# Attention and SoLU feed-forward in one kernel: the order of the PV matmuls, and mask matmuls over the whole array

## The chip, the cores and the metric

The kernel runs on one core of a Trainium2 chip. The metric is the device time of one execution in microseconds. Three executions took 211.36, 210.92 and 211.4 us; their median is 211.36. A core has the engines TensorE (PE, matmul), VectorE (DVE), ScalarE (ACT), GpSimd (POOL) and SyncE (SP, which here issues DMA transfers).

## What is computed

The reference has two parts. The first is attention with a block mask, for 4 batches, 8 heads, 768 tokens and a head size of 64:

```
scores = q @ k.T / sqrt(64)
mask: blocks of 32 tokens; a pair of blocks is kept if the blocks are at most one apart,
      if either is the first or the last block, or if the key block is among
      the three sampled blocks of the query block
attn = softmax(where(mask, scores, -1e9)); x = attn @ v
```

The second part takes the heads of a token side by side (512 numbers) and computes

```
h = x @ w_in                      # 512 -> 1024
solu = h * softmax(h)
out = layernorm(solu) * g @ w_out # 1024 -> 512
```

## The kernel before, in words

**Attention.** The 768 tokens of a head are six chunks of 128. Heads are worked in pairs. q and k are cast to bf16 and transposed, so that kT and qT hold the 64 head dimensions on partitions 0 to 63. On partitions 64 to 87 lie 24 more rows, one for each block: in kT a one-hot of the key's block, in qT the mask row of the query's block (0, or -30000 for a block that is left out). So a score matmul over 88 rows adds the mask by itself. These rows come from two small tiles that are made once at the start: `selq`, which says to which block each of the 768 tokens belongs, and `maskq`, the 24 x 24 mask of blocks. Two matmuls of line 353 spread the mask over tokens for the first head pair (24 columns of weights, 256 and 512 columns of data), and six of line 371 do it for all other tiles (128 columns of weights, 24 columns of data each). Both contract over the 24 blocks alone. The zeros and ones behind these tiles are written by memsets of VectorE at line 311.

A unit of attention (`attend`) is one batch, one head pair and one query tile of 256 queries. It has three steps. In each, four score matmuls (line 504, 256 columns each) fill an `sbank` of PSUM with the scores of four key chunks, and one instruction of ScalarE (line 515) takes the exponential of all 1024 columns into an `ex` tile [128 keys, 4 chunks, 256 queries]. Then three PV steps multiply by V. Step n has eight matmuls (line 525): for each of its four chunks m, and for each half a of the 256 queries, the weights are the 128 x 128 piece of `ex`, the moving data are the V tile of the chunk (64 values and a one for the sum, 65 columns), and the result is added to one of four places of 65 columns in an `mbank` of PSUM, one for each half and head. The V tiles of a batch lie end to end in `va` [128, 8 heads, 6 chunks, 65] in bf16, 130 bytes each. The chunk number runs over both heads of the pair: 4n + m from 0 to 11 is head (4n + m) // 6, chunk (4n + m) % 6. There are 48 units, so 576 score matmuls, 144 exponentials and 1152 PV matmuls. VectorE then divides by the sum (lines 536 and 539) into x.

**Feed-forward.** `feed` takes x of 256 tokens, transposes it (by DMA, or at line 555 on PE), computes h with matmuls of 512 columns (line 580), exponential (589), product and statistics on the other engines, transposes again, and multiplies by w_out with matmuls of 512 columns (line 636). VectorE or ScalarE scales the result (647, 650) and SP stores it.

**The order.** Nothing runs in the order of the loops. `op` records each piece of work with its engine, a guess of its cost, its dependencies and a due time. `Plan.run` then simulates the five engines with these guesses, and among the pieces that are ready on an engine takes the one that is due first; the pieces are emitted in the order of the simulated starts. A PV step enters as one piece of 8 x 0.0293 us, whatever its inner order. Memsets enter at 0.1 us each. Before the first matmul of line 580, idle time of PE in the simulation is filled with filler matmuls (line 703), at 0.9 of the idle time.

**Slots.** Scores rotate over two or three sbanks, PV and all other small results over two mbanks, `ex` over nine tiles.

Of the kernel before, what the change touches and what calls it, by code (L numbers as in the profile page):

```python
# [8 lines left out]
BF16 = mybir.dt.bfloat16  # L9
I32 = mybir.dt.int32  # L10
AX = mybir.AxisListType
ALU = mybir.AluOpType
ACT = mybir.ActivationFunctionType
# [9 lines left out]
def act_us(n, sbuf=False):  # L23
    return (n + 60 + (52 if sbuf else 0)) / 1200
# [31 lines left out]
class Plan:  # L56
# [14 lines left out]
    def op(self, eng, us, emit, deps=(), due=0.0, take=None, last_of=(), load=None, after=()):  # L71
        o = Op(eng, us, emit, deps, due, take, last_of, load, after)
        for d in {id(d): d for d in o.deps + o.after}.values():
            d.next.append(o)
            o.open += 1
        for a, name in o.last_of:
            a.held[name][0] += 1
        self.ops.append(o)
        return o
# [75 lines left out]
def kernel(  # L155
# [11 lines left out]
    nc = tc.nc  # L167

    B, H, S, D = q.shape
    BLK = 32  # L170
    NB = S // BLK
    NR = sampled_blocks.shape[1]
    P = 128
    NCH = S // P
# [10 lines left out]
    DM = D + NB  # L185

    const = ctx.enter_context(tc.tile_pool(name="const", bufs=1))
    psum = ctx.enter_context(tc.tile_pool(name="psum", bufs=1, space=PSUM))

    SPARE = 0.9  # L190
    NST, NKB, NEX, NX, NE, NSO, NSOT, NXT, NOT = 4, 3, 9, 6, 2, 3, 3, 2, 3

    def bufs(name, shape, dt, n):
# [3 lines left out]
    kT = bufs("kT", [P, NPR, 2, S], BF16, 2)  # L197
    qT = bufs("qT", [P, NPR, 2, S], BF16, 2)
    va = bufs("va", [P, H, NCH, D + 1], BF16, 2)
# [5 lines left out]
    exb = bufs("ex", [P, 4, TW], BF16, NEX)  # L205
# [37 lines left out]
    op = plan.op  # L243
# [3 lines left out]
    def bank(o, dt=FP32):  # L247
        t = mbank[o.slot]
        return t if dt == FP32 else t.bitcast(dt)
# [7 lines left out]
    def xbar_us(tiles):  # L257
# [6 lines left out]
        out=samp_i.rearrange("a b c -> a (b c)"),  # L264
        in_=bass.AP(tensor=_t32, offset=0, ap=[[2 * NR, NB], [1, 2 * NR]])), due=-100, load=0.01)
# [3 lines left out]
        out=g8, in_=moe_g_ln.rearrange("(c p) -> c p", p=P)), due=-99.5, load=0.01)  # L269
# [30 lines left out]


    oneh = const.tile([P, NCH, NB], BF16, name="oneh")
    selq = const.tile([NB, NCH, P], BF16, name="selq")
    static = const.tile([NB, NB], FP32, name="static")
    kbi = const.tile([NB, NB], I32, name="kbi")
    anyeq = const.tile([NB, NB], FP32, name="anyeq")
    maskq = const.tile([NB, NB], BF16, name="maskq")
    flat = lambda t: t.rearrange("p a b -> p (a b)")

    def fill(t, val, due):  # L310
        return op("DVE", 0.1, lambda o: nc.vector.memset(t, val), due=due)  # L311

    m1, oh1 = fill(onesf, 1.0, -2200), fill(oneh, 1.0, -2199)
    mid, stz, last = fill(ident, 0.0, -2198), fill(static, 0.0, -2197), fill(anyeq, 0.0, -2196)

    def sel(t, us, fill, base, cm, pat, deps, cmp=ALU.is_ge):
# [7 lines left out]
            due=-2194)  # L324

    stat = io
    for args in ((-NEG, 1, -1, [[1, NB]]), (-NEG, 1, 1, [[-1, NB]]), (0.0, -1, 1, [[0, NB]]),
                 (0.0, NB - 2, -1, [[0, NB]])):
        stat = sel(static, 0.12, *args, [stat, stz])
    for c in (0, NB - 1):  # L330
        stat = op("POOL", 0.08, lambda o, c=c: nc.gpsimd.memset(static[:, c : c + 1], 0.0), [stat], due=-2194)
    idf = op("DVE", 0.1, lambda o: nc.vector.tensor_copy(out=identf, in_=ident[0:KF, 0:KF]), [mids, stage[("k", 0, 1)]], due=15)
    for r in range(NR):
        last = op("DVE", 0.24, lambda o, r=r: nc.vector.scalar_tensor_tensor(
            out=anyeq, in0=kbi, scalar=samp_i[:, r, 0:1], in1=anyeq, op0=ALU.is_equal, op1=ALU.max),
            [last, io, samp_dma], due=-2089)
    mq = op("DVE", 0.24, lambda o: nc.vector.scalar_tensor_tensor(
        out=maskq, in0=anyeq, scalar=1.0, in1=static, op0=ALU.subtract, op1=ALU.mult), [last, stat], due=-2088)

    def selq_tr(o):  # L340
        for c in range(NCH):
# [1 line left out]
                             start=(c == 0), stop=(c == NCH - 1))  # L343

    sqt = op("PE", NCH * 0.056, selq_tr, [ohs, mids], due=-2190, take="m")
    sqs = op("ACT", 0.75, lambda o: nc.scalar.copy(out=flat(selq), in_=bank(sqt, BF16)[0:NB, 0:S]), [sqt],
             due=-2189, last_of=[sqt])


    krow = [op("DVE", 0.36, lambda o, hh=hh: nc.vector.tensor_copy(out=kT[0][D:DM, 0, hh, :], in_=flat(selq)), [sqs],  # L350
               due=(-2087.5, -2079.8)[hh]) for hh in range(2)]
    mps = lambda o: bank(o)[0:NB]
    mmq = [op("PE", (hi - lo) * 0.00043, lambda o, lo=lo, hi=hi: nc.tensor.matmul(  # L353
# [22 lines left out]
    for i in (1, 2, 0):  # L376
        filled["k"].append(op("ACT", 0.38, lambda o, i=i: nc.scalar.copy(
            out=kb[i][:, :, :, D:DM],
            in_=oneh.rearrange("p (o c) b -> p o c b", o=1).broadcast_to([P, 2, NCH, NB])), [ohs], due=-2075))
        filled["q"].append(op("DVE", 0.4, lambda o, i=i: nc.vector.tensor_copy(  # L380
            out=qb[i][:, :, :, D:DM],
            in_=bank(mmm)[:, 0 : NCH * NB].rearrange("p (o c b) -> p o c b", o=1, c=NCH)
            .broadcast_to([P, 2, NCH, NB])), [mmm], due=-2076, last_of=[mmm]))
    vones = [op("POOL", 0.3, lambda o, i=i: nc.gpsimd.memset(va[i][:, :, :, D : D + 1], 1.0), [stat],
                due=-1900 if i == 0 else 0) for i in range(2)]
# [3 lines left out]
        out=w_in_sb[:, c : c + 2], in_=moe_w_in.rearrange("(c p) f -> p c f", p=P)[:, c : c + 2]),  # L389
        [stage[("k", 0, 3)]], due=-2000 + c, load=3.2) for c in (0, 2)]  # L390
    w_out_load = []
    for i in range(3):
        w_out_load.append(op("SP", 0.5, lambda o, i=i: nc.sync.dma_start(
            out=hold[i], in_=moe_w_out.rearrange("(c p) d -> p c d", p=P)[:, 3 * i : min(3 * i + 3, KF)]),
            due=-43.4 + 0.1 * i, load=2.3, deps=w_in_load[:1], after=[stage[("v", 0, 3)]] + w_out_load[-1:]))
# [7 lines left out]
        out=w_out_sb[:, c, :], in0=w_out_f[c], scalar1=g_sb[:, c : c + 1], scalar2=None,  # L403
        op0=ALU.mult), [w_out_load[c // 3], gc], due=26) for c in range(KF)]
# [89 lines left out]
    def attend(b, t, pr, A):  # L494
        i = b % 2
        got, vc, later = ready[(b, pr)]
        need = [got[hh] + later.get((hh, min(t, 1)), []) for hh in range(2)]
        exs = []
        for n in range(3):
            def score(o, n=n):  # L500
                s = sbank[o.slot]
                for m in range(4):
                    hh, jc = divmod(4 * n + m, NCH)
                    nc.tensor.matmul(s[:, m, :], kT[i][0:DM, pr, hh, jc * P : (jc + 1) * P],  # L504
                                     qT[i][0:DM, pr, hh, t * TW : (t + 1) * TW],
                                     start=(m % 2 == 0), stop=(m % 2 == 1))

            so = op("PE", 4 * 0.1087, score, need[0] + (need[1] if n else []), due=A + 0.9 * n,
                    take="s")
            last_use.setdefault((b, pr), []).append(so)  # L510
            if n == 0 and 1 <= b < B - 1:

                l = NPR * t + pr
                plan.follow(stage[("kqv"[l % 3], b + 1, l // 3)], so)
            exs.append(op("ACT", act_us(1024), lambda o, so=so: nc.scalar.activation(  # L515
                out=exb[o.slot], in_=sbank[so.slot], func=ACT.Exp, scale=scale), [so], due=A + 0.9 * n,
                take="ex", last_of=[so]))
        pv0 = None
        for n in range(3):
            def pv(o, n=n, pv0=pv0):  # L520
                acc = bank(pv0 or o)[:, 0 : 4 * (D + 1)].rearrange("p (a h d) -> p a h d", a=2, h=2)
                for m in range(4):
                    hh, jc = divmod(4 * n + m, NCH)
                    for qt in range(2):
                        nc.tensor.matmul(acc[:, qt, hh, :],  # L525
                                         exb[exs[n].slot][:, m, qt * P : (qt + 1) * P],
                                         va[i][:, 2 * pr + hh, jc, :], start=(n + m + qt == 0),
                                         stop=(n == 2 and m == 3 and qt == 1), skip_group_check=True)

            pvo = op("PE", 8 * 0.0293, pv, exs + [vc], due=A + 2.2 + 0.9 * n, take=None if n else "m",  # L530
                     last_of=[exs[n]], after=[pv_last] if n else [])
            pv0 = pv0 or pvo
            pv_last = pvo
        last_use.setdefault(("pv", b, pr), []).append(pvo)
        acc = lambda: bank(pv0)[:, 0 : 4 * (D + 1)].rearrange("p (a h d) -> p a h d", a=2, h=2)
        rc = op("DVE", 0.18, lambda o: nc.vector.reciprocal(out=rb[o.slot], in_=acc()[:, :, :, D : D + 1]),  # L536
                [pvo], due=A, take="r")
        fresh = (b, t) not in x_of
        nrm = op("DVE", 0.41, lambda o: nc.vector.tensor_tensor(  # L539
            out=xb[x_of[(b, t)].slot][:, :, 2 * pr * D : (2 * pr + 2) * D].rearrange(  # L540
                "p a (h d) -> p a h d", h=2),
            in0=acc()[:, :, :, 0:D], in1=rb[rc.slot].broadcast_to([P, 2, 2, D]), op=ALU.mult),
            [rc] + ([] if fresh else [x_of[(b, t)]]), due=A,
            take="x" if fresh else None, last_of=[pv0, rc])
        if fresh:
            x_of[(b, t)] = nrm
        x_done.setdefault((b, t), []).append(nrm)
# [125 lines left out]
    for b in range(B):  # L673
        for pr in range(NPR if b == 1 else 0):

            for nm, t in (("k", kT), ("q", qT)):
                mask_rows[(nm, pr)] = op("DVE", 0.75, lambda o, t=t, pr=pr: nc.vector.tensor_copy(
                    out=t[1][D:DM, pr], in_=t[0][D:DM, 0]),
                    (krow if nm == "k" else list(qrow.values())) + w_in_load[:1] + (wo if pr > 1 else []),
                    due=Q[NPR + pr] - 5)  # L680
# [18 lines left out]
    with tc.manual_schedule():  # L699
        for o in order:  # L700
            if o.eng == "PE" and o.start <= begin:
                for _ in range(max(0, int((o.start - idle) * SPARE / (0.107 if o.start < COLD else 0.0535)))):
                    nc.tensor.matmul(flat(sbank[2])[:, 0:P], onesf, onesf, start=True, stop=True)  # L703
# [32 lines left out]
```

The softmax here doesn't subtract the row's maximum and nothing guards it: scores larger than these inputs give would overflow.

## Time and profile before

| what | value |
|---|---|
| median of three runs | 211.36 us |
| the profiled execution, its own time | 211.36 us |
| its span, first to last instruction | 209.6 us |
| PE busy, share of the span | 204.5 us, 98% |
| ACT busy | 174.1 us, 83% |
| DVE busy | 152.7 us, 73% |
| DMA queue of the loads and stores (q1), share of 16 engines' span | 77.8% |
| L525, PV matmuls | 1152, mean 194 ns each by the profile's modelled ends |
| L504, score matmuls | 576, mean 278 ns each |
| L371 and L353, mask matmuls | 6 and 2, mean 180 and 507 ns each |

How to read it. PE is the matmul part of TensorE, PEld its weight loads, which overlap the matmuls. The ends of matmuls are modelled and run past the start of the next one; what counts on PE is the distance from one start to the next. "L525" is line 525 of the kernel; a group is all instructions of a line with one operation. The chain of work that ended last starts from the last instruction and goes back, at each step, to what released it or to the instruction before it on its engine; its shares say on which engine the end of the kernel hangs. In the chain and in the timeline, "x24" says that 24 instructions of a group follow each other.

### The profile page before, as it was taken

How to read it: one execution, taken by the hardware profiler on the slowest of the kernel's cores; microseconds unless marked ns; L12 is line 12 of the kernel's file. 1: busy time of each engine (PE TensorE's matmuls, PEld its weight loads, DVE VectorE, ACT ScalarE, POOL GpSimd, SP SyncE). 2: the span in 40 equal slices, each digit the busy share in tenths (PEclk: the TensorE clock that was granted, in tenths of full speed). 3: DMA queues.
4: the chain of work that ended last, by engine and by line, in shares of the span. 5: the costliest groups of instructions: out<-in, count | busy, mean ns of one | idle time of the engine just before them, and what ended most of it. 6: DMA issues, size and time to landing. Idle time of an engine off the chain costs nothing.

```text
span 209.6 us, 5885 instructions
## 1 busy us (share of the span) xinstructions
PE 204.5 (98%) x2332; PEld 146.7 (70%) x2332; DVE 152.7 (73%) x361; ACT 174.1 (83%) x215; POOL 63.4 (30%) x131
## 2 busy tenths in 40 slices
PE   7999999999999999999999999999999999999993
PEld 6589998878667678677677767776676756454442
DVE  4767689887977978756866883858896659788720
ACT  6558999999999999988999999998998937456532
POOL 5143033305453162045331116052401111323220
PEclk9999999999999999999999999999999999999998
DMA  5999988269999799298999679799721874658562
GB/s 171 338 383 354 262 301 153 79 149 229 326 230 194 225 288 176 51 267 209 221 228 260 145 225 211 147 306 260 171 84 49 137 191 51 153 124 177 153 202 100
DMA packets 71375, 41.80 MB, mean 199 GB/s; under 512 B 54316, under 2 KB 66868, under 8 KB 71348
## 3 DMA queue, kind: packets, MB, share of 16 engines
q1 hardware_dynamic: 70752, 40.38, 77.8%
q0 software_dynamic: 544, 1.05, 2.6%
q8 instruction: 18, 0.29, 0.6%
q14 instruction: 9, 0.07, 0.1%
q10 hardware_dynamic: 52, 0.00, 0.0%
HBM read 23.07 MB, written 6.29 MB: 140 GB/s over the span
## 4 chain that ended last, share of the span: by engine, by line
PE 97%; DVE 1%; ACT 0%; issue 0%; DVEq 0%; ACTq 0%
PE sbank L504 32%; PE mbank L636 20%; PE sbank L580 20%; PE mbank L525 17%; PE mbank L467 3%; PE sbank L703 3%; DVE ot L647 1%; PE sbank L467 1%; PE mbank L555 1%; PE mbank L342 0%; PE mbank L353 0%; ACT ot L650 0%; PE mbank L397 0%; PE mbank L371 0%; DVE onesf L311 0%
## 5 line engine op out<-in xcount | busy, mean ns | idle before, releaser
L515 ACT ACTIVATE ex<-sbank 128x1024 bf16<-128x1024 f32 x144 | 138.6, 1032 | 12.4 <-PE sbank L504 11.3
L504 PE MATMUL sbank<-qT,kT 88*128 88x256 bf16 x576 | 88.2, 278 | 0.0
L504 PEld LDWEIGHTS <-kT 88*128 88x128 bf16 x576 | 53.4, 99 | 23.4 <-issue 2.3
L580 PE MATMUL sbank<-w_in_sb,xT 128*128 128x512 bf16 x192 | 52.1, 379 | 0.0
L636 PE MATMUL mbank<-w_out_sb,eso 128*128 128x512 bf16 (+1 forms) x200 | 48.0, 371 | 0.5 <-DVE ot L647 0.5
L525 PEld LDWEIGHTS <-ex 128*128 128x128 bf16 x1152 | 45.0, 97 | 4.7 <-DVE x L539 0.2
L525 PE MATMUL mbank<-va,ex 128*128 128x65 bf16 x1152 | 47.2, 194 | 0.0
L593 DVE SCALAR_TENSOR_TENSOR eso<-sbank,eso 128x1024 bf16<-128x1024 f32 x24 | 29.3, 1221 | 12.2 <-ACT eso L589 12.2
L589 ACT ACTIVATE eso<-sbank 128x1024 bf16<-128x1024 f32 x24 | 24.8, 1035 | 12.0 <-PE sbank L580 4.6
L636 PEld LDWEIGHTS <-eso 128*128 128x128 bf16 x200 | 18.8, 97 | 15.5 <-issue 0.6
L606 DVE BATCH_NORM_STATS2 bn<-eso 128x6 f32<-128x512 bf16 x40 | 25.6, 682 | 0.2
L580 PEld LDWEIGHTS <-xT 128*128 128x128 bf16 x192 | 17.9, 98 | 10.3
L613 POOL TENSOR_SCALAR mv<-se,mv 128x1 f32<-128x1 f32 x24 | 7.0, 291 | 54.3 <-DVE mv L609 43.6
L536 DVE RECIPROCAL r<-mbank 128x4 f32<-128x4 f32 x48 | 8.5, 178 | 18.9 <-PE mbank L525 18.5
L647 DVE TENSOR_SCALAR ot<-mbank,rs 128x512 f32<-128x512 f32 (+1 forms) x19 | 14.0, 734 | 11.4 <-PE mbank L636 5.7
L539 DVE TENSOR_TENSOR x<-mbank,r 128x256 bf16<-128x256 f32 x48 | 19.9, 418 | 0.7
L486 POOL CAST va<-vst 128x768 bf16<-128x768 f32 x16 | 13.7, 856 | 17.3 <-DMA vst<-in_v_dram 12.1
L421 POOL CAST kb<-kst 128x768 bf16<-128x768 f32 x12 | 10.2, 848 | 22.2 <-DMA kst<-in_k_dram 19.8
L617 POOL TENSOR_TENSOR rs<-mv,neg_half 128x1 f32<-128x1 f32 x24 | 14.2, 591 | 6.6 <-ACT ot L650 3.5
L421 POOL CAST qb<-qst 128x768 bf16<-128x768 f32 x12 | 9.9, 823 | 12.7 <-DMA qst<-in_q_dram 8.3
L597 DVE TENSOR_SCALAR eso<-eso,mu 128x1024 bf16<-128x1024 bf16 x24 | 12.6, 528 | 0.2
L611 POOL TENSOR_TENSOR se<-se 128x1 f32<-128x1 f32 x24 | 4.9, 203 | 23.9 <-ACT eso L589 23.8
(74 smaller groups left out, 121.0 us busy)
## 6 DMA issues: line engine op xcount, KB each, us to landing
vst<-in_v_dram SPq DMA_DIRECT2D x16, 384.0 KB, 4.9
out_dram<-ot SPq DMA_DIRECT2D x23, 256.0 KB, 2.4
kst<-in_k_dram SPq DMA_DIRECT2D x15, 384.0 KB, 5.5
qst<-in_q_dram SPq DMA_DIRECT2D x15, 384.0 KB, 5.4
w_in_sb<-in_moe_w_in_dram POOLq DMA_DIRECT2D x2, 512.0 KB, 11.2
kT<-in_moe_w_out_dram SPq DMA_DIRECT2D x1, 768.0 KB
qT<-in_moe_w_out_dram SPq DMA_DIRECT2D x1, 768.0 KB, 12.4
eso<-in_moe_w_out_dram SPq DMA_DIRECT2D x1, 512.0 KB
```

The source lines that it names most:

```text
L421: nc.gpsimd.tensor_copy(out=half(cb[o.slot], 0).rearrange("p (c h d) -> p c h d", c=NCH, h=2), in_=st[ld.slot].rearrange("p h c d -> p c h ...
L504: nc.tensor.matmul(s[:, m, :], kT[i][0:DM, pr, hh, jc * P : (jc + 1) * P], qT[i][0:DM, pr, hh, t * TW : (t + 1) * TW], start=(m % 2 == 0), ...
L515: exs.append(op("ACT", act_us(1024), lambda o, so=so: nc.scalar.activation(out=exb[o.slot], in_=sbank[so.slot], func=ACT.Exp, scale=scale) ...
L525: nc.tensor.matmul(acc[:, qt, hh, :], exb[exs[n].slot][:, m, qt * P : (qt + 1) * P], va[i][:, 2 * pr + hh, jc, :], start=(n + m + qt == 0) ...
L539: nrm = op("DVE", 0.41, lambda o: nc.vector.tensor_tensor(out=xb[x_of[(b, t)].slot][:, :, 2 * pr * D : (2 * pr + 2) * D].rearrange("p a (h ...
L580: nc.tensor.matmul(h[:, f * 512 : (f + 1) * 512], xTb[xp.slot][:, a, c, :], w_in_sb[:, c, f * 512 : (f + 1) * 512], start=(c == 0), stop=( ...
L589: se = op("ACT", act_us(d_ff) + 0.22, lambda o, h0=h0: nc.scalar.activation(out=eb[o.slots["e"]], in_=pair(h0), func=ACT.Exp, accum_out=se ...
L593: so = op("DVE", 1.3, lambda o, h0=h0, se=se: nc.vector.scalar_tensor_tensor(out=sob[o.slot], in0=pair(h0), scalar=1.0, in1=eb[se.slots["e ...
L606: bn = op("DVE", 2 * 0.68, lambda o, so=so: [nc.vector.bn_stats(out=bnb[o.slot][:, f], in_=sob[so.slot][:, f * 512 : (f + 1) * 512]) for f ...
L617: rs = op("POOL", 0.55, lambda o, mv=mv: nc.gpsimd.tensor_tensor(out=rsb[o.slot], in0=mvb[mv.slot][:, 0:1], in1=neg_half, op=ALU.pow), [q2 ...
L636: nc.tensor.matmul(bank(o0 or o)[:, 0:w], sotb[st.slot][:, f, :], w_out_sb[:, f, col : col + w], start=(f == 0), stop=(f == KF - 1))
L647: nc.vector.tensor_scalar(out=otb[o.slot][:, 0:w], in0=bank(o0)[:, 0:w], scalar1=rsb[rs.slot], scalar2=None, op0=ALU.mult)
```

## The change

The eight matmuls of a PV step get another order: query half 0 first with chunks 3, 2, 1, 0, then query half 1 with chunks 3, 2, 1, 0. Before, chunk 0 came first, with half 0 and half 1, then chunk 1, and so on. The start and stop flags move to the first and last matmul of the new order. The tiles `selq` and `maskq` get 128 partitions in place of 24; two new memsets on VectorE write zeros to them, and the mask lands in the first 24 partitions. The copies of `selq` into kT read the first 24 partitions as before. The mask matmuls of lines 353 and 371 take the whole tiles, so they contract over 128 rows, of which 104 are zero.

```diff
+    PV_ORDER = [(3 - m, a) for a in range(2) for m in range(4)]
...
-    selq = const.tile([NB, NCH, P], BF16, name="selq")
+    selq = const.tile([P, NCH, P], BF16, name="selq")
...
-    maskq = const.tile([NB, NB], BF16, name="maskq")
+    maskq = const.tile([P, NB], BF16, name="maskq")
...
+    sqz, mqz = fill(selq, 0.0, -2195.9), fill(maskq, 0.0, -2195.8)
...
-        out=maskq, in0=anyeq, scalar=1.0, in1=static, op0=ALU.subtract, op1=ALU.mult), [last, stat], due=-2088)
+        out=maskq[0:NB], in0=anyeq, scalar=1.0, in1=static, op0=ALU.subtract, op1=ALU.mult), [last, stat, mqz], due=-2088)
...
-    sqs = op("ACT", 0.75, lambda o: nc.scalar.copy(out=flat(selq), in_=bank(sqt, BF16)[0:NB, 0:S]), [sqt],
+    sqs = op("ACT", 0.75, lambda o: nc.scalar.copy(out=flat(selq)[0:NB], in_=bank(sqt, BF16)[0:NB, 0:S]), [sqt, sqz],
...
-                for m in range(4):
+                for k, (m, qt) in enumerate(PV_ORDER):
                     hh, jc = divmod(4 * n + m, NCH)
-                    for qt in range(2):
-                        nc.tensor.matmul(acc[:, qt, hh, :],
-                                         exb[exs[n].slot][:, m, qt * P : (qt + 1) * P],
-                                         va[i][:, 2 * pr + hh, jc, :], start=(n + m + qt == 0),
-                                         stop=(n == 2 and m == 3 and qt == 1), skip_group_check=True)
+                    nc.tensor.matmul(acc[:, qt, hh, :], exb[exs[n].slot][:, m, qt * P : (qt + 1) * P],
+                                     va[i][:, 2 * pr + hh, jc, :], start=(n + k == 0),
+                                     stop=(n == 2 and k == 7), skip_group_check=True)
```

More of the change, by code (lines that the diff above doesn't have):

```diff
@@ L345 @@
     sqt = op("PE", NCH * 0.056, selq_tr, [ohs, mids], due=-2190, take="m")
-    sqs = op("ACT", 0.75, lambda o: nc.scalar.copy(out=flat(selq), in_=bank(sqt, BF16)[0:NB, 0:S]), [sqt],
+    sqs = op("ACT", 0.75, lambda o: nc.scalar.copy(out=flat(selq)[0:NB], in_=bank(sqt, BF16)[0:NB, 0:S]), [sqt, sqz],
              due=-2189, last_of=[sqt])
-    krow = [op("DVE", 0.36, lambda o, hh=hh: nc.vector.tensor_copy(out=kT[0][D:DM, 0, hh, :], in_=flat(selq)), [sqs],
+    krow = [op("DVE", 0.36, lambda o, hh=hh: nc.vector.tensor_copy(out=kT[0][D:DM, 0, hh, :], in_=flat(selq)[0:NB]), [sqs],
                due=(-2087.5, -2079.8)[hh]) for hh in range(2)]
```

## The prediction, made before the result was known

> **What bounds the kernel now.** I read the page first: the busy shares and the chain that ended last.
>
> ```profile
> PE 204.5 (98%) x2332; PEld 146.7 (70%) x2332; DVE 152.7 (73%) x361; ACT 174.1 (83%) x215; POOL 63.4 (30%) x131
> ...
> PE 97%; DVE 1%; ACT 0%; issue 0%; DVEq 0%; ACTq 0%
> PE sbank L504 32%; PE mbank L636 20%; PE sbank L580 20%; PE mbank L525 17%; PE mbank L467 3%; PE sbank L703 3%; DVE ot L647 1%; PE sbank L467 1%; PE mbank L555 1%; PE mbank L342 0%; PE mbank L353 0%; ACT ot L650 0%; PE mbank L397 0%; PE mbank L371 0%; DVE onesf L311 0%
> ```
>
> TensorE carries 97% of the chain, and the PV matmuls (L525), which the change reorders, are 17% of it: about 35 us. A busy PE can still be a waiting PE, so I read next who waits for whom.
>
> ```profile
> DVE r L536 <- PE mbank L525: 18.5, 22, 2.5
> ...
> ACT ex L515 <- PE sbank L504: 11.3, 26, 1.3
> ...
> PE mbank L636 <- DVE ot L647: 0.5, 1, 0.5
> ```
>
> The columns are us in total, times, longest. Others wait for PE; PE's own longest named wait is 0.5 us. The stage that could take a gain back is the one where ScalarE's exps are dense, so I cut the span into stretches.
>
> ```profile
> 60.00:80.00 20.00, 20.00 (x260) 14.69 (x257) 16.96 (x40) 19.12 (x24) 7.91 (x15) 1.00 0.98 226
> ...
> 120.00:140.00 20.00, 20.00 (x254) 14.87 (x252) 13.28 (x33) 19.38 (x24) 6.56 (x12) 1.00 0.91 218
> ...
> 150.00:160.00 10.00, 10.00 (x116) 6.98 (x115) 7.01 (x18) 10.00 (x13) 2.89 (x8) 1.00 0.28 66
> ```
>
> After the length come PE, its weight loads, VectorE, ScalarE and GpSimd. ScalarE is busy 19.1 to 19.4 of 20 us: close behind PE, but behind, except in 150 to 160 where it is full. The chain in order of time then gives what one matmul really costs on the path.
>
> ```profile
> 10.29 0.85 PE sbank L504 x4
> 11.14 0.26 PE mbank L371 x6
> ...
> 44.88 1.25 PE mbank L525 x40
> ...
> 52.18 0.88 PE sbank L504 x8
> ```
>
> So 40 PV matmuls take 1.25/40 = 31.2 ns each. What they should take I get from single start times in the trace: score matmuls with 256 columns follow each other at 108 to 109 ns, output matmuls with 512 at 215 to 216. That is 107/256 = 0.418 ns a column and some 1.5 ns beside; 65 columns would be 28.7 ns.
>
> The same start times say where the rest is. I took the 1152 starts of L525 from the trace by their place in the step of eight (chunk m, query half a). From the first half's start to the second's it is 33.3 ns, from the second half's to the next chunk's 29.2: the eight means are 32.2, 30.9, 32.8, 29.1, 33.3, 29.1, 33.2, 29.1, together 31.2. So PV alternates between a clean 29.2 and a delayed 33.3.
>
> Which matmul is delayed? A V tile is 65 bf16, 130 bytes, so chunk tiles lie end to end and start at every even offset within 16 bytes. I joined the starts to the addresses that the program gives. Where the first half's tile starts inside the 16 bytes in which the last tile ended, the interval is 33 (471 of 471, within 31 to 36). Where it starts on a multiple of 16 (35 times directly after another chunk), it is 29, and then the repeat of that tile has 35. Of the 504 other repeats 494 are clean; 7 have 32 to 34, and three waited longer. In 11 steps whose first tile follows a matmul of L555, L580 or L636 and does not start on 16 bytes, the first is clean too. My reading: the delay belongs to reading on from where the last read ended, and sometimes to reading the same tile again; a tile that is neither is clean.
>
> **The change, part by part.** It is summed against the profiled execution: span 209.6, time 211.36, so 1.76 us lie around the span; 211.36 is also the median of the three runs.
>
> PV order. Nothing is added or removed: 1152 matmuls with as many weight loads, same waits, same planner cost. With half outer and chunks going down, no two neighbours have the same tile, and none reads on upward. If my reading holds, all become clean: 1152 x (31.2 - 29.15) = 2.36 us of PE time.
>
> What takes some back? ScalarE's exps wait for scores 11.3 us in all, 4.4 of it between 30 and 160 us, while some 920 matmuls and so 1.9 us of the gain lie in that stretch. The waits are short and spread: ScalarE runs 2 to 11 us, mostly, then waits 0.1 to 0.6, and a run of 5 us spans some five PV steps, which gain 5 x 8 x 2.05 = 82 ns. So most gaps hold it. Not those of the full stretch 150 to 160 and of one run of 15 us at 33.7; I take off 0.25 for them and for late DMA or GpSimd work that follows PE. Remains 2.1 us.
>
> What this doesn't show: neighbours now accumulate onto the same 65 PSUM columns 29 ns apart, where today it is 62 ns. Nearest rows: L636 adds eight times to the same 512 columns at 216 ns, the fillers of L703 overwrite one place every 56 ns, both without a delay. Bounds: nothing, or one delay of 4.2 ns for each of the 16 same-place neighbours in 24, 768 x 4.2 = +3.2 us; below nothing is excluded, since the clean 29.2 is already counted. I take nothing, by the L703 row, and keep the upper end in the slower rival.
>
> [...]
>
> Mask matmuls. Those of L371 (24 rows, 6 x 24 columns) sit in a hole:
>
> ```profile
> 10.08 1.06 PE L504 MATMUL sbank<-qT,kT 88*128 88x256 bf16 x4
> 11.07 0.33 PE L371 MATMUL mbank<-maskq,selq 24*128 24x24 bf16 x6
> 11.33 0.39 PE L703 MATMUL sbank<-onesf 128*128 128x128 bf16 x2
> ```
>
> L504's four starts are 0.213 apart, so it ends at 10.93; L371 starts 0.14 later; its last start is 11.225, its 24 columns take 0.02, and L703 comes 0.09 after. Elsewhere, L504 to an L467 of 128 x 88, both over the whole array, there is no gap. Over all rows L371 would lose both: 0.23 us, at the half clock of this stretch (0.85/4 = 213 ns a score here, 0.88/8 = 110 later, though the page's clock row shows 9 from the start). [...] L353 keeps its 24 columns and its gaps of 0.14 and 0.13: 0, at best -0.2.
>
> Fills. Two memsets of VectorE at 1.33 us, behind anyeq. Nearest rows: ident, 64 words, 0.11; onesf 128 and oneh 144 elements, 0.165 and 0.178, so about 1 ns an element. selq costs 0.4 to 0.8 us, maskq 0.06. VectorE idles until 2.89, so it is free. Behind them waits `warm`, whose exp runs at 3.04 after a table load; the copy into selq, which now waits for its memset, starts at 3.16. Without that cover it would be up to 0.9 us. The planner books 0.1 us each; I followed its early times by hand: the warm exp ends 0.2 later, the selq copy 0.01, and by 6 us all is as before. So I expect the same order and fillers.
>
> The clock. [...] Here the rise at 17.1 comes 5.8 us after the last hole, which is L371's own. [...] From the rows I can't tell whether a hole as short as L371's matters: I take 0, and keep -1.0.
>
> Sum: 2.1 + 0.15 = 2.25, so 211.36 - 2.25 = 209.1.
>
> **The rivals.** *Nothing moves in PV*: the delay is a rate, 62.5 ns for two matmuls by some unit that doesn't care about order. For it: the pair sum is 62 to 64 also where the delay sits on the repeat. Against: the delay returns to its place after each aligned tile, where a rate would keep its new phase. Time: the mask part only, 211.2.
>
> *Slower*: the delay belongs to each matmul whose tile is not its predecessor's, and the repeat is the cheap one. Now half are repeats; afterwards none, so all 1152 take 33.3: (33.3 - 31.2) x 1152 = +2.4, less 0.15: 213.6. It decides from the first PV at 18.3 us on, since PE has no slack. For it: in most pairs the new tile is the delayed one. Against: the 35 aligned and 11 fresh tiles are new and clean, though behind a long matmul a fetch could be hidden. A PSUM delay would end here too.
>
> **How the numbers follow.** Forecast 0.63, nothing 0.20, slower 0.17. Forecast's own range 208.1 (clock) to 209.9 (half the delays stay). The range reaches to 211.9, over the second case, and leaves out the slower one. A measurement tells some 0.3%, 0.6 us, from no change: faster 0.63, same 0.20, slower 0.17.
>
> **What would show it.** A PV block of 24 in the chain takes 0.70 instead of 0.75; L525's share falls from 17% to 16; all starts are 29 apart; L371 follows L504 without a hole; L504's and L580's counts and order stay; ScalarE's wait for L504 shrinks below 11.3. Wrong if L525 intervals stay at 31 or go to 33, or if PE shows new waits for ScalarE that eat the gain.

## The result, and the profile after

The changed kernel takes 207.11 us (median of 38 runs, 206.26 to 208.43). The kernel before, run beside it, takes 210.99 us (43 runs, 206.93 to 211.82). The forecast was 209.1 with a range of 208.1 to 211.9: the direction was right, the time lies below the range.

The times of the kernel before fall into two groups, near 207.5 and near 211.4, and the ratio of 0.9975 (95% interval 0.9961 to 0.9989) compares the changed kernel with the lower group alone. With the runs beside the experiments, the kernel before ran 185 times: 102 times at 206.6 to 209.2 (median 207.59) and 83 times at 210.2 to 212.0 (median 211.41). All 38 runs of the changed kernel lie in the lower group. So the change does two things: it removes the upper group, which is worth 3.8 us in 45% of the executions, and it takes some 0.25% off the rest. The three runs that I predicted from (211.36, 210.92, 211.4) were all from the upper group, and so was the profile.

The page after, busy shares and chain:

```profile
span 204.9 us, 5887 instructions
...
PE 199.4 (97%) x2332; PEld 142.9 (70%) x2332; DVE 153.4 (75%) x363; ACT 173.9 (85%) x215; POOL 64.1 (31%) x131
...
PE 93%; DVE 4%; ACT 0%; issue 0%; DVEq 0%; ACTq 0%
PE sbank L508 30%; PE mbank L638 20%; PE sbank L582 20%; PE mbank L528 17%; PE mbank L471 2%; PE sbank L705 2%; DVE w_out_sb L406 2%; DVE qT L364 1%; PE mbank L557 1%; PE sbank L471 1%; DVE qT L479 0%; PE mbank L346 0%; DVE ot L649 0%; DVE kb L449 0%; DVE kT L479 0%
```

The lines of the kernel have moved: L504 is now L508, L525 L528, L353 L357, L371 L375, L703 L705. The same 2332 matmuls follow in the same order; two memsets are new. PE is busy 5.1 us less, and the chain now runs in part over VectorE: in the first 10 us over its copies into qT and kT, and once more from 28 to 32 us.

Where did 4.7 us of span go? The timeline of PE at the start of the kernel after, in order of time (start, length to the modelled end of the last one, line, shapes, count):

```profile
6.08 0.50 PE L705 MATMUL sbank<-onesf 128*128 128x128 bf16 x3
6.38 0.76 PE L508 MATMUL sbank<-qT,kT 88*128 88x256 bf16 x4
7.07 0.52 PE L471 MATMUL mbank<-ident,kb 128*64 128x128 bf16 x6
7.52 0.61 PE L508 MATMUL sbank<-qT,kT 88*128 88x256 bf16 x4
8.06 0.52 PE L471 MATMUL mbank<-ident,qb 128*64 128x128 bf16 x6
8.52 0.29 PE L705 MATMUL sbank<-onesf 128*128 128x128 bf16 x2
8.64 0.60 PE L508 MATMUL sbank<-qT,kT 88*128 88x256 bf16 x4
9.07 0.30 PE L375 MATMUL mbank<-maskq,selq 128*128 128x24 bf16 x6
9.23 0.27 PE L705 MATMUL sbank<-onesf 128*128 128x128 bf16 x2
```

Before, the groups of four score matmuls took 1.03 to 1.06, and it went on so to 17.1 us:

```profile
5.34 0.81 PE L353 MATMUL mbank<-selq,maskq 24*24 24x256 bf16 x2
...
15.14 1.06 PE L504 MATMUL sbank<-qT,kT 88*128 88x256 bf16 x4
...
17.07 0.63 PE L504 MATMUL sbank<-qT,kT 88*128 88x256 bf16 x4
```

Now the second group takes 0.61: the clock record of the trace has PE at full clock from 6.7 us on, where before it was 17.1. And the hole is gone: L375 starts 0.108 after the last score matmul, one clean interval, and the six take 0.16 where they and their gaps took 0.40.

The first PV block starts at 13.84 in the chain, before at 18.47: a lead of 4.6 us. The block of 40 starts at 40.85, before at 44.88: 4.0. At the end of the span it is 4.7. So some 0.8 (the 0.6 and what PV gained meanwhile) is given back between 14 and 41 us. The largest piece is one wait of 0.5 us of PE, before the PV matmuls at 32.02. The chain shows what it waited for:

```profile
28.32 2.24 DVE w_out_sb L406 x4
30.56 0.09 DVE r L538
30.65 0.98 DVE w_out_sb L406
31.63 0.34 DVE x L541
31.98 0.04 issue
32.02 0.65 PE mbank L528 x16
```

VectorE multiplies g into w_out (L406), and the x of an earlier unit, which frees the `mbank`, stands behind it. Three of these instructions take 1.03 to 1.06 us here, where the three of the same form took 0.45 to 0.48 before. Here each runs beside a cast of GpSimd; the casts wait for loads that land at the same time as before (the first cast starts at 29.41, before at 29.25), while PE and VectorE are 4.6 us further on. That the casts slow VectorE is not shown by a run of its own. From 41 us on 0.7 is gained. One PV block, in the chain after:

```profile
40.85 1.22 PE mbank L528 x40
...
45.79 0.73 PE mbank L528 x24
```

40 took 1.25 before, 24 took 0.75. A block of 24 was foretold at 0.70. Over all PV matmuls in the trace the mean interval, from the start of one to the start of the next matmul, is 30.55 ns against 31.22 (waits of over 60 ns left out).

The memsets cost what a 384-word and a 12-word fill cost, ahead of idle time:

```profile
1.36 0.38 DVE L313 MEMSET selq<- 128x384 uint32 x1
1.69 0.07 DVE L313 MEMSET maskq<- 128x12 uint32 x1
1.71 0.06 DVE L273 MEMSET warm<- 1x1 f32 x1
2.89 0.50 DVE L338 SCALAR_TENSOR_TENSOR anyeq<-kbi,samp_i,anyeq 24x24 f32<-24x24 int32 x2 [1.12 <-POOL static L321]
```

### The profile page after: what moved, and what is told of

Read it like the earlier page. It is cut to its first block, busy times and chain, and to the rows that moved or that the text cites. A ratio compares the mean times of both kernels' runs of the same rounds, so it can differ in the third digit from the quotient of the medians.

```text
span 204.9 us, 5887 instructions
## 1 busy us (share of the span) xinstructions
PE 199.4 (97%) x2332; PEld 142.9 (70%) x2332; DVE 153.4 (75%) x363; ACT 173.9 (85%) x215; POOL 64.1 (31%) x131
## 4 chain that ended last, share of the span: by engine, by line
PE 93%; DVE 4%; ACT 0%; issue 0%; DVEq 0%; ACTq 0%
PE sbank L508 30%; PE mbank L638 20%; PE sbank L582 20%; PE mbank L528 17%; PE mbank L471 2%; PE sbank L705 2%; DVE w_out_sb L406 2%; DVE qT L364 1%; PE mbank L557 1%; PE sbank L471 1%; DVE qT L479 0%; PE mbank L346 0%; DVE ot L649 0%; DVE kb L449 0%; DVE kT L479 0%
## 5 line engine op out<-in xcount | busy, mean ns | idle before, releaser
L508 PE MATMUL sbank<-qT,kT 88*128 88x256 bf16 x576 | 85.6, 272 | 0.0
L508 PEld LDWEIGHTS <-kT 88*128 88x128 bf16 x576 | 52.5, 97 | 22.8 <-issue 2.1
L528 PEld LDWEIGHTS <-ex 128*128 128x128 bf16 x1152 | 44.3, 98 | 5.4 <-issue 0.5
L528 PE MATMUL mbank<-va,ex 128*128 128x65 bf16 x1152 | 46.5, 194 | 0.3 <-DVE x L541 0.3
L490 POOL CAST va<-vst 128x768 bf16<-128x768 f32 x16 | 14.3, 894 | 20.9 <-DMA vst<-in_v_dram 19.7
## 6 DMA issues: line engine op xcount, KB each, us to landing
w_in_sb<-in_moe_w_in_dram POOLq DMA_DIRECT2D x2, 512.0 KB, 11.3
```

What stands on the lines that cost most here:

```text
L490: vc = op("POOL", pool_us(S) + 0.3, lambda o: nc.gpsimd.tensor_copy(out=va[i][:, 2 * pr : 2 * pr + 2, :, 0:D], in_=vst[ld.slot]), [ld, von ...
L528: nc.tensor.matmul(acc[:, qt, hh, :], exb[exs[n].slot][:, m, qt * P : (qt + 1) * P], va[i][:, 2 * pr + hh, jc, :], start=(n + k == 0), sto ...
```

## The experiments

My theory after the result: the mask edit lets the clock rise early in all executions, because the mask matmuls of L353, at 5.3 to 6.1 us, now work on all rows in the stretch ahead of the rise at 6.7 (A1); the PV order is worth about 0.5 us. Rivals: the hole of L371 decides (A2), the PV order decides (B), the count of cells or columns in use decides (A3). For what is left of the PV delays: reading upward (R1), a change of the place in PSUM (R2), or a rate. Some expectations speak of a window of 3.4 us. It is read from the clock records: from its rise to its fall, full clock lasts 191.15 us in the trace before and 197.97 in the one after, 6.83 apart, which is twice 3.41.

### Which part: the mask edit alone, and the PV order alone

The mask edit alone is the changed kernel with the old PV loop:

```diff
-                for k, (m, qt) in enumerate(PV_ORDER):
+                for m in range(4):
+                    for qt in range(2):
```

> The whole mask edit, with PV in its old order. Times of the kernel before lie in two groups, near 207.5 and near 211.3. Theory A (the mask edit lets TensorE's clock rise early, within the first 7 us, in every execution; the PV order is worth 0.5): all times at 207.5 to 207.8, none above 209, L525 as before at 31.2 ns, and in the profile the score matmuls at half rate end near 7 us. Theory B (the PV order brings the change): two groups as before, with a quarter or more of the times above 210.

Measured: 207.57 us (206.97 to 208.09, 6 runs), all in the lower group; full clock from 4.5 us on; PV 31.2 ns. The ratio to the lower group of before is 0.9992 (0.9967 to 1.0016): in an execution whose clock rises early, the mask edit is worth nothing that can be measured.

The PV order alone is the kernel before with the new loop.

> The new PV order alone, mask matmuls over 24 rows. Theory A: two groups again, each 0.5 lower than before: about 206.9 and 210.8, a third or more of the times in the upper one; PV intervals of 30.7 ns on average. Theory B: one group near 207.

Measured: 207.13, 206.18 and 207.18 in the lower group, 211.14, 210.68 and 210.8 in the upper; ratio of the lower ones 0.9957 (0.9924 to 0.9989). The profile is of the upper group: full clock from 17.5 us, PV 30.6 ns. B falls.

### Which of the two mask matmuls

L353 alone over all rows, from the mask edit alone:

```diff
-            nc.tensor.matmul(bank(o)[:, c * NB : (c + 1) * NB], selq[:, c, :], maskq, start=(c == 0),
+            nc.tensor.matmul(bank(o)[:, c * NB : (c + 1) * NB], selq[0:NB, c, :], maskq[0:NB], start=(c == 0),
```

> Old PV order; only the two mask matmuls of L353 take 128 rows, those of L371 keep 24 rows and their hole of 0.23 us. L353's start times are the same before and after the change, so it has the same holes. Theory A1 (what counts is how many rows of the array a busy window works on, and L353 sits in the first window): one group at 207.6 to 207.9. Theory A2 (what counts is the hole around L371): two groups, near 207.5 and 211.3.

Measured: 207.92 us (207.24 to 208.11, 6 runs), one group; full clock from 6.1 us. With the odds of the kernel before, six of six would come 0.55^6 = 3 times in 100.

L371 alone over all rows:

```diff
-        mps(o)[:, 0 : hi - lo], maskq, flat(selq)[:, lo:hi], start=True, stop=True), [mq, sqs], due=due, take="m")
+        mps(o)[:, 0 : hi - lo], maskq[0:NB], flat(selq)[0:NB, lo:hi], start=True, stop=True), [mq, sqs], due=due, take="m")
```

> Old PV order; only the six mask matmuls of L371 take 128 rows, L353 keeps 24. Theory A1: two groups, near 207.4 and 211.2. Theory A2: one group near 207.5. If both edits are needed, two groups here and in the run of L353 alone.

Measured: five runs of six at 206.78 to 207.75, one at 210.37. That tells too little, so I ran it again with more runs.

> L371 over 128 rows, L353 over 24, once more, because five of the first six times were in the lower group and one at 210.4 was not. Theory A1 (L353 decides whether the clock rises early): about half of the times in an upper group. The upper group sits lower than that of the kernel before (210.8 to 211.9), near 210.4, if closing the hole of L371 lets the clock rise one window of 3.4 us earlier. Theory A2: at most one in ten above 209.

Measured: 9 of 22 in the lower group, 13 at 209.71 to 210.64 (median 210.23), and the profile is one of these. The timeline of its PE (the fillers are L707 here):

```profile
5.67 0.81 PE L357 MATMUL mbank<-selq,maskq 24*24 24x256 bf16 x2
...
10.41 1.06 PE L508 MATMUL sbank<-qT,kT 88*128 88x256 bf16 x4
11.27 0.36 PE L375 MATMUL mbank<-maskq,selq 128*128 128x24 bf16 x6
11.47 0.37 PE L707 MATMUL sbank<-onesf 128*128 128x128 bf16 x2
11.64 1.06 PE L508 MATMUL sbank<-qT,kT 88*128 88x256 bf16 x4
...
13.24 0.62 PE L508 MATMUL sbank<-qT,kT 88*128 88x256 bf16 x4
```

Half clock to 13.3, full clock after, where the late profiles with L371 over 24 rows have 17.1 to 17.5: by this one profile L371's 24 rows and their hole do hold the clock back, but later; the lower group keeps about its share (14 of 28 with the first six, 102 of 185 before), so L371 doesn't decide which group a run falls into. The upper group sits 1.2 us below that of before. A1 stands, A2 falls as the main cause.

### Rows, or cells in use

The kernel before, with 128 columns of weights for L353 and still 24 rows:

```diff
-    maskq = const.tile([NB, NB], BF16, name="maskq")
+    maskq = const.tile([NB, P], BF16, name="maskq")
...
-        mps(o)[:, 0 : hi - lo], maskq, flat(selq)[:, lo:hi], start=True, stop=True), [mq, sqs], due=due, take="m")
+        bank(o)[:, 0 : hi - lo], maskq, flat(selq)[:, lo:hi], start=True, stop=True), [mq, sqs], due=due, take="m")
```

> The kernel before, but L353's two matmuls get 128 columns of weights (zeros past the 24) and keep their 24 rows; L371 as before. The cells of the array in use are as many as with 128 rows and 24 columns. Theory A1, rows count: two groups again, near 207.5 and 211.3, each time with even odds. Rival A3, cells or columns in use count: one group near 207.6, and a clock rise before 8 us in the profile.

Measured: 13 of 22 in the lower group, 9 at 210.75 to 211.43. 24 rows by 128 columns don't help, 128 rows by 24 columns do (none of six late with L353 alone): A3 falls. The profile is of the lower group, and it shows when the clock is early in spite of 24 rows (L353 is L354 here, L504 L505):

```profile
5.03 0.49 PE L354 MATMUL mbank<-selq,maskq 24*128 24x256 bf16 x2
6.06 0.60 PE L505 MATMUL sbank<-qT,kT 88*128 88x256 bf16 x4 [0.26 <-ACT qT L361]
```

Full clock came at 4.6 us, ahead of the mask matmuls. That is the pattern of all profiles here: with 24 (or 64) rows in L353 it comes at 4.6 or 4.8, before L353 starts, or at 13.3 to 17.5; with 128 rows it comes at 4.5, 4.9, 5.0, 6.1, 6.5, 6.5, 6.7 or 7.1, before or after L353.

Then 64 rows:

```diff
-        mps(o)[:, 0 : hi - lo], maskq, flat(selq)[:, lo:hi], start=True, stop=True), [mq, sqs], due=due, take="m")
+        mps(o)[:, 0 : hi - lo], maskq[0:64], flat(selq)[0:64, lo:hi], start=True, stop=True), [mq, sqs], due=due, take="m")
```

> Old PV order, L371 over 24 rows; L353 over 64 rows in place of 24 or 128. It tells how the clock's rise depends on the rows in use. If every used row counts in proportion, L353's 0.75 us count as half, and fewer times than half fall into the upper group near 211.3. If only nearly full rows count, half of them do, as in the kernel before. If any count over 24 is enough, none does.

Measured: 4 of 15 in the upper group (211.18 to 211.65; profile at 17.5 us). Two of the three cases fit: by the odds of the kernel before, 4 or fewer of 15 would come about one time in eight. 64 rows are not enough in every execution; what the traces say of a proportion follows under "Why two groups?".

### What delays a PV matmul

All of these have the whole mask edit. First the chunks going up:

```diff
-    PV_ORDER = [(3 - m, a) for a in range(2) for m in range(4)]
+    PV_ORDER = [(m, a) for a in range(2) for m in range(4)]
```

> The changed kernel with the chunks of a half going up (0, 1, 2, 3) in place of down; the half stays outer, mask edit whole. Theory R1 (a delay where the moving V tile lies above the one just read): nearly every neighbour reads on upward, so the mean PV interval rises to about 31.9 ns and the time by 1.3 us over the changed kernel, to 208.4. Theory R2 (a delay where the output goes to another of the four places in PSUM, at most one in two matmuls): places change as in the changed kernel, so 30.5 ns and 207.1.

Measured: 208.22 us (22 runs; two of them at 209.98 and 211.33), PV 32.3 ns. Of the 938 matmuls whose tile follows the last one in memory, 900 have 32 ns or more to the next start; of the other 38, 35 are all those whose tile starts on a multiple of 16 bytes, with 29 or 30. The 144 that jump down by three tiles are all at 29 or 30. A block of 24 in the chain:

```profile
70.34 0.77 PE mbank L528 x24
```

R2 falls: the places in PSUM change as in the changed kernel, which has 0.73. Reading on within 16 bytes costs some 4 ns nearly every time in this run (900 of 903). Adding to the same place as the matmul before shows no cost: in the changed kernel 768 matmuls do so, with 30.0 ns on average, against 31.5 for the others that follow a PV matmul.

Then pairs of halves, chunks going down:

```diff
-    PV_ORDER = [(3 - m, a) for a in range(2) for m in range(4)]
+    PV_ORDER = [(3 - m, a) for m in range(4) for a in range(2)]
```

> The changed kernel with the chunk outer and going down and the two halves of a chunk next to each other: (3,0) (3,1) (2,0) (2,1) and so on. Theory R1: only the step boundaries read upward, so about one delay in eight, 29.7 ns on average, and 206.1. Theory R2: the place changes at every matmul as in the old order, so 31.2 ns and 207.6, the time of the mask edit alone.

Measured: 207.17 us (206.32 to 208.71, 17 runs), PV 30.6 ns: neither 29.7 nor 31.2. Places change at every matmul, so R2 falls again; but R1 alone should have given more. The delays are now mostly on the repeats of a tile that doesn't start on 16 bytes: 167 of 504 have 32 ns or more.

Then aligned tiles, order as in the changed kernel:

```diff
-    va = bufs("va", [P, H, NCH, D + 1], BF16, 2)
+    va = [t[:, :, :, 0 : D + 1] for t in bufs("va", [P, H, NCH, 72], BF16, 2)]
```

> The changed kernel with V tiles 144 bytes apart in place of 130, so that each starts on a multiple of 16 bytes. Theory R1 in the prediction's form (only a tile that starts in the 16 bytes where the last one ended is delayed): the jumps up at half and step boundaries become clean, so about 29.5 ns (what is left follows score matmuls) and 206.2. Theory R2: nothing changes, 30.5 ns and 207.1.

Measured: 206.73 us (206.52 to 207.72, 16 runs), PV 30.5 ns. No tile can share 16 bytes with its neighbour, jumps up by three tiles are mostly clean (103 + 28 of 144 at 29 or 30), and still there is a delay: one of 35 ns in about every five matmuls, wherever it falls. Three kernels without the upward read inside a half or a pair end at 30.55, 30.56 and 30.49. None tried with 65 columns comes below some 30.5 ns. For its time I ran the aligned tiles again:

> The changed kernel with V tiles 144 bytes apart, once more, for its time: 16 runs gave 206.73 where the changed kernel gave 207.11 in other runs, with the same 30.5 ns a PV matmul. If the two are the same kernel in time, 206.9 to 207.3 here and a ratio to the kernel before that overlaps 0.9975; if the alignment is worth something, 206.7 again.

Measured: 206.97 us (206.16 to 207.5, 22 runs), ratio 0.9971 (0.9957 to 0.9985), against 0.9975 for the changed kernel: no difference that can be told. No version that clearly beats the changed kernel came out.

Last, tiles of 64 columns:

```diff
-    va = bufs("va", [P, H, NCH, D + 1], BF16, 2)
+    va = bufs("va", [P, H, NCH, D], BF16, 2)
...
-                    nc.tensor.matmul(acc[:, qt, hh, :], exb[exs[n].slot][:, m, qt * P : (qt + 1) * P],
+                    nc.tensor.matmul(acc[:, qt, hh, 0:D], exb[exs[n].slot][:, m, qt * P : (qt + 1) * P],
```

> The changed kernel with V tiles of 64 columns, 128 bytes, end to end: each fills eight pieces of 16 bytes and shares none. The last of the 64 value columns gives way to the ones for the sum, so one output dimension of each head is left out; all else is as in the changed kernel. The changed kernel, the pairs going down and the tiles 144 bytes apart all ended at 30.5 ns a matmul, with one delay of 6 ns in some five matmuls. Theory F1 (this floor is the reading of nine pieces for 65 columns): with eight the floor goes, 28.8 ns clean, about 29.0 on average with what follows score matmuls, time down by 1.5 us to about 205.5. Theory F2 (the floor is the weight loads, or another rate per matmul): the mean stays at 30.3 to 30.5 and the time at 206.7 to 207.1.

Measured: 205.88 us (205.63 to 206.0, 4 runs), PV 29.6 ns. A block in the chain:

```profile
69.93 0.71 PE mbank L528 x24
```

The delays of 35 are gone; the intervals are 28 to 30, one like the other. One column less explains 0.4 of the 0.9 ns, by the 0.418 ns a column that the prediction takes from its rows. So F1 holds in part: the recurring delay of 6 ns comes with the 65th column. But the 29.0 that F1 expects is not reached, and what holds the remaining 0.6 ns was not tried.

## Why the prediction was wrong, point by point

**The clock: the step that failed.** The prediction put it so: "From the rows I can't tell whether a hole as short as L371's matters: I take 0, and keep -1.0." And of the other mask matmuls: "L353 keeps its 24 columns and its gaps of 0.14 and 0.13: 0, at best -0.2." So the clock's term was put at nothing, and laid to the wrong matmul. Measured, it is 3.8 us (211.41 against 207.59) where the clock rises late, and the matmul is L353, two matmuls that take 0.8 us together, whose holes the change doesn't touch. I looked only for gaps in time, and by gaps L353 is the same before and after (it starts at 5.34 and at 5.33 us); what differs is the rows in use, 24 and 128. The rows of before held the hint: L353 with 24*24 at 5.34 us, and half clock to 17.1. Of L371's part the direction was seen: without its 24 rows and their hole the clock comes at 13.3 in place of 17.1 to 17.5, and the upper group is 1.2 us lower, where I took 0. The -1.0 that the lower end of the range keeps for the clock is shown by no run; the runs showed that 1.2 for L371 alone, and 3.8 for the whole mask edit where the clock had risen late.

**Why two groups?** From its rise to its fall at the end of the kernel, full clock lasts 191.15, 194.56, 197.97 or 201.39 us in the 14 traces, and that is 56, 57, 58 or 59 times 3.413 us. The rises themselves, at 4.5 to 17.5 us, share no place in such steps counted from the first instruction. I assumed that the same steps lie ahead of a rise too and that the work in one step decides on the rise at its end; no trace shows either by itself. Such steps, counted back from each rise, are called windows here. For each window I summed the time in which matmuls stream their columns at half clock (213 ns for 256, so 0.83 ns a column), as it is, weighted by the rows in use of 128, and weighted by the cells in use:

| share of a window of 3.413 us | the 14 windows that end with a rise | the 24 before them that end after PE's first matmul |
|---|---|---|
| time | 0.78 to 1.00 | at most 0.93 |
| time, weighted by rows | 0.78 to 0.89 | at most 0.74 |
| time, weighted by cells | 0.45 to 0.78 | at most 0.65 |

Of the three, only the weighting by rows separates the two columns. In the kernel before, the window with L353 has 0.70, the next 0.72, the one with L371 0.71, and the one that ends at 17.1 has 0.89. With L371 over all rows its window has 0.80 and ends with the rise at 13.3. An estimate from this: if the windows may begin anywhere in the trace of before and 0.75 is enough, the rise is late in 45% of cases (42 to 51% for limits of 0.74 to 0.78); with 64 rows in L353 it would be late in 10 to 37%, with 128 never. Measured: 83 of 185, 4 of 15, and 2 of 131 runs of the seven kernels whose L353 has 128 rows (209.98 and 211.33, both of the kernel with chunks going up; no profile shows what they were). So rows in proportion fit all the runs. But the limit is read from the same traces, it separates them only if the record of the rise is within some 0.1 us of a window's end, and no run tests it apart.

**The base.** I took the profiled execution for the kernel, because the three times agreed. They were one of two groups; that three of three fall into it happens about one time in eleven (0.45 to the third). The profile had a sign of it: PE at half rate for 17 us (213 ns from one score matmul to the next, 108 to 109 later), although fillers stand in its gaps.

**PV order.** The delay for reading on upward was read rightly, and is real (the chunks going up, 32.3 ns). But "If my reading holds, all become clean: 1152 x (31.2 - 29.15) = 2.36 us" was three times too large. Measured, 1152 x (31.22 - 30.55) = 0.77 us of PE time, of which 0.25% or 0.5 us shows in the time. No order tried held the clean 29.15 (30.49 is the lowest with 65 columns): without that delay another appears, 5 to 6 ns in about every fifth matmul. In the changed kernel 225 matmuls after another PV matmul have 33 ns or more, and 114 of these are among the 218 that jump up by three or seven tiles, between halves and between steps, which the prediction didn't count as reading on. With tiles on multiples of 16 bytes these jumps are mostly clean, and the delay falls elsewhere. The rival "the delay is a rate" was therefore right for a part: no order tried came below 30.5. The prediction had a sign of it, the 35 on repeats of aligned tiles, and gave that rival 0.20.

**What takes some back.** 0.25 was taken off for ScalarE and late DMA or GpSimd work. ScalarE's waits for scores fell from 11.3 to 6.4 us, as foretold; the larger price, 0.8 us, was paid between 14 and 41 us, where PE had come further ahead than the sum foresaw, and 0.5 of it waiting for VectorE, which the sum didn't have. The chunks going up cost 1.97 us of PE time over the changed kernel, and 1.1 us of time.

**The hole of L371.** With L371 alone over all rows, still at half clock, its six matmuls and their gaps take 0.20 us in place of 0.40; 0.23 was foretold. The 0.15 that the sum has for it is shown by no run: in the late group L371 alone over all rows gave 1.2 us, with an earlier rise of the clock. Where the clock rises early, the whole mask edit shows no gain (ratio 0.9992).

**The sum.** 3.8 us were missed at the clock and 1.6 too many forecast for PV (2.1 against 0.5). The two errors partly cancel: that 209.1 is only 2.0 us off is luck. In the range, too, half of the delays staying would give 209.1 + 1.18 = 210.3, and not 209.9; the measured time lies at the other end.

**PSUM.** Taken as nothing, with an upper end of 3.2 us. The runs bear the nothing out: the kernel with chunks going up and the changed one change their place in PSUM at the same matmuls, and the first has 32.3 ns, the second 30.55.

**The slower rival** (any new tile is delayed) would have had 33.3 ns; 30.55 was measured. **Fills** and **the order**: as predicted, 0.45 us ahead of idle time, and the same order on all engines.

## What to carry to other kernels

Ask what a matmul that uses few rows costs beyond its own time. Here two of them with 24 rows, 0.8 us together, went with half rate for some 10 us more (a rise at 17 us in the profile in place of 4.5 to 7; 3.8 us of time, in 45% of the executions), and zeros in the unused rows repaired that for the price of two memsets, 0.45 us ahead of idle time of VectorE. Before a sum is made on a profile, ask whether the runs have more than one level, and look at the first microseconds for the rate of single matmuls. For small matmuls, take the start times apart by address: the order in which tiles are read cost up to a tenth of each here (32.3 against 29.15 ns), but removing one delay may only uncover the next limit, here some 30.5 ns.

## What the runs showed of the hardware that was not expected

- With L353 over 128 rows x 24 columns 2 of 131 runs were late (none of six with L353 alone, none of 38 of the changed kernel); over 24 x 128, the same count of cells, 9 of 22 were, and over 24 x 24, 83 of 185. So in these runs the rows in use went with an early rise of the clock, and the cells did not. The extra rows held zeros.
- Full clock lasted 56 to 59 times 3.413 us in every trace here (191.15 to 201.39 us), with rises at 4.5 to 17.5 us that share no place in such steps from the first instruction. If the steps are counted back from the rise, the one before it has 0.78 or more by rows in all 14 traces, and none of the 24 earlier ones has over 0.74.
- In the kernel with chunks going up, a matmul of 65 columns whose moving tile starts in the 16 bytes where the last tile ended takes some 4 ns longer to the next start (32 ns or more in 900 of 903); one whose tile starts on a multiple of 16 bytes (35 of 35) or jumps down by three tiles (144 of 144) has 29 to 30.
- In the orders without such delays, 65 columns still take some 30.5 ns on average, by one delay of 5 to 6 ns in about five matmuls; at 64 columns in 128 bytes this is gone (29.6 ns).
- A change between the score matmuls, which have 88 rows, and others, which have 128, went with 4 to 5 ns more to the next start in the traces before and after, at full clock: the first PV matmul after a score matmul has a median of 34 ns (52 and 53 of them), after an output or h matmul 29 or 30 (14 and 14); the first h matmul after a score matmul has 220 (44 and 44) where 215 or 216 is usual, and the first score matmul after a PV matmul a median of 113 or 114 (41 and 42) where 108 is. That the rows are the reason is not shown by a run of its own.
